# A preLN attention and gated-MLP layer on one core: half of chunk 2's q·k products summed in pairs of tiles by an accumulating transfer, with a new order of steps

## The chip, the cores and the metric

The kernel runs on one core of a Trainium2 chip. The metric is the device time of one execution in microseconds (us), lower is better. It is compared as a median of several runs on the same chip.

## What is computed

```
h  = x + A(layernorm(x))            x: 2048 x 512, bf16
h2 = h + B(layernorm(h))
A: q,k,v = x @ wqkv                 32 heads of 16
   logits[s,w] = q[s] . k[s-2w] / 4      w = 0..7, positions below 0 masked
   o[s] = sum_w softmax(logits)[s,w] v[s-2w];   A = o @ wo
B: gate = x @ W_gate; up = x @ W_up      512 -> 1376
   B = (relu(gate) * up) @ W_down        1376 -> 512
```

## The kernel before

The 2048 positions are cut into four chunks of 512 (`tk` 0 to 3). For each chunk the steps are the same: layernorm, transpose, projection to q, k and v (TensorE, L584), products q·k for eight shifts (VectorE, L635 or L650), sum of these products over the 16 numbers of a head (TensorE, matmul with a matrix `sel` of ones and zeros: "scores", L641, L672 or L693), exponential (L707), denominators (L724), spread of the weights over partitions (eight small transfers per chunk from SyncE, L767), products with v (VectorE, L799 or L814), a tree of additions over the eight shifts (the first level as an accumulating transfer from GpSimd, L842; later levels on VectorE, L802, L836), output projection (TensorE, L880), residual (VectorE, L891), second layernorm (L456, L509), transpose, gate and up (L953; their last 96 columns apart, L920, with a transpose by DMA at L939), and down (L1004).

q and k lie as four tiles of 128 partitions (`t` 0 to 3), where tile t holds 4 of the 16 numbers of all 32 heads. The eight shifts of a chunk are taken in two halves of four (`hf` 0 and 1). For one half VectorE makes the products in two steps of two tiles each; each fills one product buffer, `big`, of 128 x 8 x 512 (1 MB): four shifts for the two tiles. The scores then need 16 matmuls of 128 x 512 against 32 columns each, since both buffers are to be summed. For the halves of chunk 3 (`PRE`) VectorE adds the second buffer to the first (L679), and 8 matmuls do (L693).

Product buffers are scarce: there are five `big` tiles, named big_88 to big_92 below, and the q,k weights' space `wqk_sb` is a sixth once all projections are done. The products with v, the spread weights and the q·k products all draw on them.

The order is written out by a planner. Every step is an `Op` with its engine, its dependencies and its buffers, and the table `RANK` gives each step its place; the planner takes them in that order and emits each engine's instructions in it. Engines then run their queues in order; a step waits for the steps whose results it needs, and for the last reader of a buffer that it overwrites. SyncE and GpSimd only issue transfers here, in queue order too. The tuple `PRD` names the halves (chunk, half) whose two product buffers are to be added by a GpSimd transfer; it is empty before.

The weights for up (`wgu_sb`, L315) and down (`wd_sb`, L309 and L312) are loaded in the middle of the run, from SyncE, after chunk 0's attention has ended.

Of the kernel before, what the change touches and what calls it, by code (L numbers as in the profile page):

```python
# [15 lines left out]


RANK = [
# [38 lines left out]
]  # L57


# [142 lines left out]
def kernel(  # L202
# [22 lines left out]
    BCD = {(0,0):"SSSS",(0,1):"SSSS",(1,0):"SSSS",(1,1):"SSSS",(2,0):"SSSS",(2,1):"SSSS",(3,0):"SSSS",(3,1):"SSSS"}  # L225
    PRE = ((3,0),(3,1))
    PRE2 = ()
    PRD = ()
    ODA = (0, 1)
    LATE = "ud"  # L230
    NAB = 0
# [335 lines left out]
    for tk in range(NCK):  # L567
# [53 lines left out]
        for hf in range(2):  # L621
            sc, ex = Buf(at_s), Buf(ex_s)
            scd, prd = [], []
            for t in range(0, NT, 2):
# [32 lines left out]
                else:  # L657
# [3 lines left out]
                    prd.append((a, pb, f_sc))  # L661
            if (tk, hf) in PRD:
                def f_pd(p0=prd[0][1], p1=prd[1][1]):
                    nc.gpsimd.dma_start(p0.t[:], p1.t[:], accum_op=ALU.add, max_dma_last_dim=4096)
# [429 lines left out]
```

## Time and profile before

| | us |
|---|---|
| median of 3 runs | 192.64 |
| lowest, highest | 192.41, 193.5 |
| the profiled execution, its own time | 193.63 |
| its span, first to last instruction | 191.8 |
| TensorE busy | 185.8 (97%) |
| VectorE busy | 148.3 (77%) |
| ScalarE busy | 115.1 (60%) |
| transfers, 16 engines: SyncE's queue, GpSimd's queue | 30.8%, 25.0% of the span |

All times in this document that have a place ("at 74.05") count from the start of the span. PE is TensorE, DVE VectorE, ACT ScalarE, POOL GpSimd, SP SyncE. Rows of a timeline have start, length, engine, line, operation and tiles, and a count where like instructions in a row were merged; the length of a merged row goes from the first start to the last end. A clock of 1.00 is the full TensorE clock, which the trace shows throughout (mean 0.999).

### The profile page before, as it was taken

Reading aid. Unit: us, or ns where it says so; the run is one execution under the profiler, and the core shown is the slowest. Engines: PE = TensorE matmul, PEld = TensorE weight load, DVE = VectorE, ACT = ScalarE, POOL = GpSimd, SP = SyncE. Lnnn points to the kernel's source line nnn. Section 1 sums busy time; section 2 is a strip of 40 time slices with the busy share of each in tenths; the row PEclk is TensorE's granted clock in tenths of the full one; section 3 lists DMA queues with packets and bytes.
Section 4 is the critical chain, followed back from the end, with each engine's and each line's share of the span. In section 5 each row is a group of like instructions: output and inputs, shape, how many; then the busy total and the mean of one; then the engine's idle time right before and its main releaser. Section 6 shows DMA issues by size and latency. Waiting matters only on the chain.

```text
span 191.8 us, 3035 instructions
## 1 busy us (share of the span) xinstructions
PE 185.8 (97%) x1101; PEld 96.9 (51%) x1120; DVE 148.3 (77%) x230; ACT 115.1 (60%) x236; POOL 18.5 (10%) x35
## 2 busy tenths in 40 slices
PE   7799999999999999999999999999999999999994
PEld 7695455554445354544355444444446444444653
DVE  5799999999999999999999988999627500232433
ACT  2479989997644885793174597615468600656600
POOL 3000002320000033000153000033001000000000
PEclk9999999999999999999999999999999999999999
DMA  5799365993078979628599906689503450000063
GB/s 185 259 329 386 74 158 117 178 191 72 0 198 208 371 157 197 116 43 202 111 166 190 195 20 144 153 157 173 103 0 55 84 164 3 0 27 0 14 215 103
DMA packets 26719, 26.45 MB, mean 138 GB/s; under 512 B 12528, under 2 KB 22608, under 8 KB 26704
## 3 DMA queue, kind: packets, MB, share of 16 engines
q1 hardware_dynamic: 23248, 16.39, 30.8%
q0 software_dynamic: 2736, 8.91, 25.0%
q10 hardware_dynamic: 720, 0.95, 1.6%
q8 instruction: 9, 0.15, 0.3%
q14 instruction: 6, 0.05, 0.1%
HBM read 8.42 MB, written 2.10 MB: 55 GB/s over the span
## 4 chain that ended last, share of the span: by engine, by line
PE 93%; DMA 3%; DVE 1%; issue 1%; SPq 0%
PE bank L953 36%; PE bank L584 21%; PE bank L1004 20%; PE bank L880 7%; DMA x_sm<-in_A_x_dram 3%; PE bank L641 3%; PE bank L920 3%; PE bank L543 2%; PE bank L693 1%; PE bank L724 0%; SPq L323 0%; DVE st L466 0%; DVE row L514 0%; DVE row L1012 0%; DVE mv L469 0%
## 5 line engine op out<-in xcount | busy, mean ns | idle before, releaser
L953 PE MATMUL bank<-quad,wgu_sb 128*128 128x512 bf16 x310 | 71.3, 379 | 0.5
L953 PEld LDWEIGHTS <-wgu_sb 128*128 128x128 bf16 x320 | 30.9, 98 | 37.1 <-issue 1.7
L1004 PE MATMUL bank<-wd_sb,gT 128*128 128x512 bf16 (+3 forms) x195 | 39.4, 355 | 0.2
L960 ACT ACTIVATE gr<-bank 128x512 bf16<-128x512 f32 x40 | 23.5, 609 | 19.4 <-PE bank L953 15.7
L584 PE MATMUL bank<-quad,wqk_sb 128*128 128x512 bf16 (+2 forms) x173 | 30.4, 320 | 1.1 <-DVE quad L557 0.7
L957 ACT CAST up_sb<-bank 128x512 bf16<-128x512 f32 x40 | 23.0, 594 | 13.8 <-PE bank L953 8.7
L981 DVE TENSOR_TENSOR gT<-gr,up_sb 128x1024 bf16<-128x1024 bf16 x20 | 13.7, 688 | 19.4 <-ACT up_sb L957 11.6
L1004 PEld LDWEIGHTS <-gT 128*128 128x128 bf16 (+1 forms) x198 | 18.4, 98 | 19.8 <-issue 0.4
L635 DVE TENSOR_TENSOR big<-quad,kT 128x4096 bf16<-128x4096 bf16 x11 | 24.8, 2282 | 0.1
L584 PEld LDWEIGHTS <-wqk_sb 128*128 128x128 bf16 x176 | 16.9, 114 | 11.9 <-issue 2.1
L842 POOL DMA_DIRECT2D big<-big x13 | 11.8, 958 | 80.4 <-DVE big L799 47.1
L1012 DVE SCALAR_TENSOR_TENSOR row<-bank,iv,x_sm 128x512 bf16<-128x512 f32 (+2 forms) x10 | 6.2, 641 | 13.5 <-PE bank L1004 13.4
L584 PE MATMUL bank<-quad,wv_sb 128*128 128x512 bf16 x61 | 15.6, 379 | 0.2
L880 PE MATMUL bank<-wo_sb,quad 128*128 128x512 bf16 x64 | 14.8, 379 | 0.0
L456 ACT ACTIVATE junk<-x_sm,sm 128x512 bf16<-128x512 bf16 x16 | 11.6, 727 | 4.8 <-DVE x_sm L891 4.8
L799 DVE TENSOR_TENSOR big<-big,vT 128x4096 bf16<-128x4096 bf16 x6 | 13.5, 2283 | 0.2 <-DMA big<-ex 0.2
L802 DVE TENSOR_TENSOR big<-big 128x1024 bf16<-128x1024 bf16 (+2 forms) x19 | 12.2, 656 | 0.7 <-DMA big<-big 0.6
L466 DVE BATCH_NORM_STATS2 st<-x_sm 128x6 f32<-128x512 bf16 x16 | 10.2, 679 | 1.8 <-DMA x_sm<-in_A_x_dram 1.8
L559 ACT COPY quad<-bank 128x1024 bf16<-128x1024 bf16 (+1 forms) x9 | 7.6, 894 | 6.4 <-PE bank L543 6.4
L1010 ACT ACTIVATE up_sb<-bank,iv 128x512 bf16<-128x512 f32 x8 | 5.3, 689 | 10.2 <-PE bank L1004 10.2
L891 DVE SCALAR_TENSOR_TENSOR x_sm<-x_sm,bank 128x512 bf16<-128x512 bf16 x16 | 10.7, 679 | 0.5 <-PE bank L880 0.5
L592 ACT CAST quad<-bank 128x512 bf16<-128x512 f32 x16 | 9.2, 595 | 2.0 <-PE bank L584 1.9
(81 smaller groups left out, 183.9 us busy)
## 6 DMA issues: line engine op xcount, KB each, us to landing
big<-big POOLq DMA_DIRECT2D x13, 512.0 KB, 5.3
big<-ex SPq DMA_DIRECT2D x24, 128.0 KB, 2.7
wgu_sb<-in_B_W_gate_dram SPq DMA_DIRECT2D x1, 1376.0 KB, 11.0
wgu_sb<-in_B_W_up_dram SPq DMA_DIRECT2D x2, 688.0 KB, 4.2
wd_sb<-in_B_W_down_dram SPq DMA_DIRECT2D x2, 640.0 KB, 6.7
x_sm<-in_A_x_dram SPq DMA_DIRECT2D x2, 512.0 KB, 5.9
wqk_sb<-wqk_sb POOLq DMA_DIRECT2D x2, 512.0 KB, 4.8
wqk_sb<-ex SPq DMA_DIRECT2D x8, 128.0 KB, 2.7
```

The costliest lines, as they stand in the source:

```text
L456: nc.scalar.activation(out=junk[:, j % 2, :], in_=h.t[:] if h else x_sm[:, tk * BPC + j, :], func=ACT.Square, bias=sm.t[:, j:j + 1], scale ...
L584: nc.tensor.matmul(mm.t[:, lo:hi], lhsT=wv_sb[:, dt, t:D:NT] if c == 2 else wqk_sb[:, dt, c * D + t:(c + 1) * D:NT], rhs=xnT.t[:, dt, lo:h ...
L635: V.tensor_tensor(out=pb.t[:].rearrange("p (t w) s -> p t w s", t=2), in0=q4, in1=k4, op=ALU.mult)
L799: V.tensor_tensor(out=mt.t[:], in0=ab.t[:], in1=v8, op=ALU.mult)
L802: V.tensor_tensor(out=mt.t[:, 0:n, :], in0=mt.t[:, 0:n, :], in1=mt.t[:, n:2 * n, :], op=ALU.add)
L842: nc.gpsimd.dma_start(mt.t[:, 0:4, :], mt.t[:, 4:8, :], accum_op=ALU.add)
L880: nc.tensor.matmul(od.t[:], lhsT=OT.t[:, t, j * P:(j + 1) * P], rhs=wo_sb[:, t, :], start=(t == 0), stop=(t == NT - 1 and tk not in RPE))
L953: nc.tensor.matmul(mm.t[:fs, lo:hi], lhsT=wgu_sb[:, dt, g, ft * P: ft * P + fs], rhs=hnT.t[:, dt, lo:hi], start=(dt == 0), stop=(dt == NT ...
L957: nc.scalar.copy(out=ub.t[:fs, i, :], in_=um.t[:fs, :])
L960: nc.scalar.activation(out=gr.t[:fs, i, :], in_=gm.t[:fs, :], func=ACT.Relu)
L981: V.tensor_tensor(out=gt.t[:fs, 0:n, :], in0=gr.t[:fs, 0:n, :], in1=ub.t[:fs, 0:n, :], op=ALU.mult)
L1004: nc.tensor.matmul(od.t[:, c0:c1], lhsT=gts[ft].t[:fs, ft % 2, j * P:(j + 1) * P], rhs=wd_sb[:fs, ft, c0:c1], start=(ft == 0), stop=(ft == ...
```

## The change

Half 1 of chunk 2 gets the path named by `PRD`. VectorE still makes its two product buffers. A transfer issued by GpSimd (L664) then adds the second buffer to the first, 1 MB, and the scores of this half are 8 matmuls (L672) where there were 16 (L641). Everything else is computed as before. The table `RANK` is another one throughout: it has one entry more and was searched anew, so that steps on all engines stand in another order.

```
 RANK = [
-    1, 2, 3, 4, 5, 6, 7, 8, 9, 10, 18, 11, 12, 13, 14, 15, 16, 17, 0, 19,
+    0, 1, 2, 3, 4, 5, 6, 7, 8, 9, 18, 10, 11, 12, 13, 15, 16, 17, 14, 19,
...
-    PRD = ()
+    PRD = ((2,1),)
```

The branch that this turns on stood in the code before:

```
if (tk, hf) in PRD:
    def f_pd(p0=prd[0][1], p1=prd[1][1]):
        nc.gpsimd.dma_start(p0.t[:], p1.t[:], accum_op=ALU.add, max_dma_last_dim=4096)
...
    def f_sc(sc=sc, pb=prd[0][1]):
        for u in range(2):
            for g in range(4):
                nc.tensor.matmul(sc.t[g * HB:(g + 1) * HB, :], lhsT=sel[:],
                                 rhs=pb.t[:, 4 * u + g, :], start=(u == 0),
                                 stop=(u == 1), tile_position=(0, g * HB))
```

The rows below are instructions in the order of an engine's queue: line, operation, what is written and read, shape. First GpSimd's queue before, from the four first-level additions of chunk 0 to the four of chunk 1 (L842; each is named by the buffer on which it works):

```order
L842 DMA big_88<-big_88 128x2048
L842 DMA big_89<-big_89 128x2048
L842 DMA big_91<-big_91 128x2048
L842 DMA big_90<-big_90 128x2048
L842 DMA wqk_sb<-wqk_sb 128x2048
L842 DMA big_89<-big_89 128x2048
L842 DMA big_92<-big_92 128x2048
L842 DMA big_90<-big_90 128x2048
```

GpSimd's queue at the same place now:

```order
L842 DMA big_90<-big_90 128x2048
L842 DMA big_88<-big_88 128x2048
L842 DMA big_91<-big_91 128x2048
L842 DMA big_89<-big_89 128x2048
L664 DMA big_92<-big_90 128x2x2048
L842 DMA wqk_sb<-wqk_sb 128x2048
L842 DMA big_89<-big_89 128x2048
L842 DMA big_91<-big_91 128x2048
L842 DMA big_90<-big_90 128x2048
```

The new transfer stands between chunk 0's additions and chunk 1's. It reads big_90, which is also the buffer of chunk 1's last addition.

SyncE's queue before, from the loads of up's weights to the spread of chunk 2's weights (the L939 transpose belongs to chunk 0's gate and up, the first two L767 rows to chunk 1, the last two to chunk 2):

```order
L315 DMA wgu_sb<-in_B_W_up_dram 128x2x1376
L767 DMA big_88<-ex_100 128x1x512 x4
L767 DMA big_88<-ex_102 128x1x512 x4
L315 DMA wgu_sb<-in_B_W_up_dram 128x2x1376
L309 DMA wd_sb<-in_B_W_down_dram 128x5x512 x2
L312 DMA wd_sb<-in_B_W_down_dram 96x512
L939 DMA_TRANSPOSE gT_96<-row_106 128x4x128
L767 DMA wqk_sb<-ex_101 128x1x512 x4
L767 DMA wqk_sb<-ex_100 128x1x512 x4
```

SyncE's queue at the same place now:

```order
L315 DMA wgu_sb<-in_B_W_up_dram 128x2x1376 x2
L767 DMA big_88<-ex_100 128x1x512 x4
L767 DMA big_88<-ex_102 128x1x512 x4
L939 DMA_TRANSPOSE gT_93<-row_104 128x4x128
L309 DMA wd_sb<-in_B_W_down_dram 128x5x512
L312 DMA wd_sb<-in_B_W_down_dram 96x512
L309 DMA wd_sb<-in_B_W_down_dram 128x5x512
L767 DMA big_88<-ex_100 128x1x512 x4
L767 DMA big_88<-ex_101 128x1x512 x4
```

Both halves of up's weights now go ahead of chunk 1's spread, and the loads of down's weights have moved behind the L939 transpose.

VectorE's queue before, from the second product step of chunk 2's half 1 (the first L635 row), over half 0 of that chunk and the four products of chunk 1 with v (L799):

```order
L635 TENSOR_TENSOR big_89<-quad_87,kT 128x4096
L635 TENSOR_TENSOR big_90<-quad_87,kT 128x4096
L635 TENSOR_TENSOR big_91<-quad_87,kT 128x4096
L799 TENSOR_TENSOR wqk_sb<-big_88,vT 128x4096
L799 TENSOR_TENSOR big_89<-big_88,vT 128x4096
L799 TENSOR_TENSOR big_92<-big_88,vT 128x4096
L799 TENSOR_TENSOR big_90<-big_88,vT 128x4096
L981 TENSOR_TENSOR gT_93<-gr_111,up_sb_109 128x1024
L635 TENSOR_TENSOR big_91<-quad_86,kT 128x4096
L802 TENSOR_TENSOR big_89<-big_89 128x1024
L930 TENSOR_TENSOR row_106<-gr_112,bank_143 128x2x96
```

VectorE's queue at the same place now:

```order
L635 TENSOR_TENSOR big_90<-quad_87,kT 128x4096
L635 TENSOR_TENSOR big_89<-quad_87,kT 128x4096
L635 TENSOR_TENSOR big_91<-quad_87,kT 128x4096
L799 TENSOR_TENSOR wqk_sb<-big_88,vT 128x4096
L799 TENSOR_TENSOR big_89<-big_88,vT 128x4096
L799 TENSOR_TENSOR big_91<-big_88,vT 128x4096
L930 TENSOR_TENSOR row_104<-gr_112,bank_142 128x2x96
L799 TENSOR_TENSOR big_90<-big_88,vT 128x4096
L930 TENSOR_TENSOR row_104<-gr_112,bank_138 128x2x96
L739 TENSOR_TENSOR row_106<-ex_101,ex_100 128x512
L981 TENSOR_TENSOR gT_94<-gr_111,up_sb_109 128x1024
L635 TENSOR_TENSOR big_92<-quad_84,kT 128x4096
```

The two L930 rows, after which the L939 transpose can go, now stand around the last product with v, and that product writes big_90, the source of the new transfer.

74 rows, old and new, of the table RANK are left out of this document.

## Prediction

> **What bounds the kernel now.** I read the page's busy shares first, then the chain that ended last, then what TensorE waits for.
>
> ```profile
> PE 185.8 (97%) x1101; PEld 96.9 (51%) x1120; DVE 148.3 (77%) x230; ACT 115.1 (60%) x236; POOL 18.5 (10%) x35
> PE 93%; DMA 3%; DVE 1%; issue 1%; SPq 0%
> PE bank L427 <- DVE warm L327: 1.0, 1, 1.0
> PE bank L584 <- DVE quad L557: 0.7, 1, 0.7
> PE bank L584 <- DMA wqk_sb<-in_A_wqkv_dram: 0.2, 1, 0.2
> ```
>
> The last of these waits, in TensorE's timeline:
>
> ```profile
> 9.27 0.27 PE L584 MATMUL bank<-quad,wqk_sb 128*128 128x128 bf16 x2 [0.72 <-DVE quad L557]
> ```
>
> The chain is 93% TensorE, and the whole list of TensorE's waits is three entries of 1.9 us together, the last of them before 9.27. Behind them TensorE runs without a hole up to its last matmul. So an instruction that leaves TensorE shortens the time by its own length, and a step on any other engine is worth nothing until it comes so late that TensorE waits for it. VectorE is nearly as full in the middle of the run, which says where that could happen:
>
> ```profile
> 60.00:80.00 20.00, 19.89 (x127) 9.34 (x127) 19.69 (x16) 15.07 (x31) 3.45 (x4) 1.00 0.94 226
> 140.00:160.00 20.00, 19.89 (x103) 9.72 (x103) 8.04 (x20) 10.23 (x24) 0.86 (x1) 1.00 0.32 73
> ```
>
> Columns are length, then busy us of TensorE, weight load, VectorE, ScalarE, GpSimd, then clock, transfer share and GB/s. From 60 to 80, where the new transfer goes, TensorE and VectorE have no slack and the transfer engines are 94% busy; from 140 on VectorE and the transfers are mostly idle. A delay between 60 and 80 would show.
>
> **The matmuls that go.** The chain of work in order of time has one run for each half's scores:
>
> ```profile
> 62.16 0.98 PE bank L641 x16
> 65.84 0.98 PE bank L641 x16
> 95.45 0.55 PE bank L693 x8
> ```
>
> The first two are chunk 2's halves with 16 matmuls, the third a half of chunk 3 that already has 8. One half goes from the first form to the third: 0.98 - 0.55 = 0.43 us less on TensorE, all of it on the path.
>
> **The new transfer.** The trace has no 1 MB addition, but it has 512 KB ones of the same kind. GpSimd's timeline, the rate of all transfers from 66 to 82 in slices of 0.4 us with GpSimd's queue in that window, and the landing of the last of chunk 1's four additions, from issue:
>
> ```profile
> 67.45 0.86 POOL L842 DMA_DIRECT2D wqk_sb<-wqk_sb  x1 [28.02 <-DVE wqk_sb L799]
> 74.05 0.86 POOL L842 DMA_DIRECT2D big<-big  x1 [1.34 <-DVE big L799]
> GB/s 381 366 338 200 115 13 0 174 236 236 164 164 246 113 225 225 184 184 215 215 123 225 184 195 215 195 184 195 184 236 205 195 184 133 10 0 0 0 0 0
> q0 software_dynamic: 576, 2.10, 69.6%
> big<-big POOLq DMA_DIRECT2D x1, 512.0 KB, 6.2
> ```
>
> The first is issued at 67.45; the rate falls to zero at 68.4 and starts again at 68.8, so data moves some 1.4 us after issue. It stops in the slice at 79.6, and GpSimd's packets fill 69.6% of the 16 us, 11.1 us: data from 68.8 to some 79.85, 2.77 us for each 512 KB, one behind the other. The last landed at 74.05 + 6.2 = 80.25, 0.4 us after its data. So 1 MB takes 5.5 us, and 1.4 + 5.5 + 0.4 = 7.3 us from issue to landing.
>
> When is it issued, and who waits? VectorE's timeline (start, length):
>
> ```profile
> 58.27 6.68 DVE L635 TENSOR_TENSOR big<-quad,kT 128x4096 bf16<-128x4096 bf16 x3
> 64.87 2.28 DVE L799 TENSOR_TENSOR wqk_sb<-big,vT 128x4096 bf16<-128x4096 bf16 x1
> 67.07 6.68 DVE L799 TENSOR_TENSOR big<-big,vT 128x4096 bf16<-128x4096 bf16 x3
> 73.68 0.68 DVE L981 TENSOR_TENSOR gT<-gr,up_sb 128x1024 bf16<-128x1024 bf16 x1
> 78.35 0.42 DVE L739 TENSOR_TENSOR row<-ex,ex 128x512 bf16<-128x512 bf16 x1
> 80.83 0.41 DVE L836 TENSOR_TENSOR quad<-big 128x512 bf16<-128x512 bf16 x1
> 81.16 0.68 DVE L802 TENSOR_TENSOR big<-big 128x1024 bf16<-128x1024 bf16 x1
> 81.77 0.75 DVE L836 TENSOR_TENSOR quad<-big 128x512 bf16<-128x512 bf16 x2
> 82.77 0.34 DVE L930 TENSOR_TENSOR row<-gr,bank 128x192 bf16<-128x192 bf16 x1
> ```
>
> Lengths overlap the next start by 0.08 (64.87 + 2.28 against 67.07), so I take each 0.08 shorter: L635 and L799 2.20, L981 and L802 0.60, L739 0.34, L836 0.33, L930 0.26. The same VectorE steps lie ahead of the second product step of half 1 in both orders, only shuffled, so I let it start at 58.27 again and end at 60.47. GpSimd issued 0.3 to 0.4 us behind VectorE before (67.45 against the end at 67.07), so the transfer goes at 60.85, its data ends at 67.75 and it lands at 68.2, if nothing else moves. Three things can wait for it:
>
> - Its scores. The new order puts 16 matmuls of half 0, then five groups of four L953 and two of eight L920 ahead of them. The chain gives 8.80 us for 40 of the first and 0.66 us for eight of the second:
>
> ```profile
> 69.51 0.66 PE bank L920 x8
> 70.87 8.80 PE bank L953 x40
> ```
>
> Half 0's products end at 64.87 as before, so these scores start no earlier than 64.87 + 0.98 + 20 x 0.22 + 2 x 0.66 = 71.6. Spare: 3.4 us.
> - The last product with v, which overwrites the transfer's source. VectorE reaches it at 64.87 + 3 x 2.20 + 0.26 = 71.7. Spare: 3.5 us.
> - Chunk 1's four additions, next in GpSimd's queue. The first product with v ends at the same 67.07 as before, so their data would start at 68.8 again. Spare: 1.05 us.
>
> So I cost the transfer at nothing. What covers it is TensorE's work on chunk 0's gate and up. If that cover were gone, the price is 7.3 us less what lies between.
>
> **What the new order moves onto the transfer engines.** This is the doubtful term. Before, the loads of down's weights were issued at 60.6 and had nearly all landed when chunk 1's additions started to move, and the L939 transpose was issued when they were over:
>
> ```profile
> 60.61 1.14 SPq L309 DMA_DIRECT2D wd_sb<-in_B_W_down_dram  x2
> 61.80 0.69 SPq L312 DMA_DIRECT2D wd_sb<-in_B_W_down_dram  x1
> 83.14 1.23 SPq L939 DMA_TRANSPOSE gT<-row  x1
> q1 hardware_dynamic: 1450, 1.82, 102.8%
> wd_sb<-in_B_W_down_dram SPq DMA_DIRECT2D x2, 640.0 KB, 6.7
> wd_sb<-in_B_W_down_dram SPq DMA_DIRECT2D x1, 96.0 KB, 6.9
> ```
>
> Now both stand behind the last L930. VectorE ends that at 64.87 + 4 x 2.20 + 2 x 0.26 = 74.2. The transpose is issued at 74.2 (1.2 us), the loads from 75.5 to 77.3: 1376 KB, in the middle of chunk 1's last two additions. The fourth line is SyncE's queue from 62 to 67, loads alone: 1.82 MB in 5 us, 364 GB/s, so the loads are worth 3.9 us of all engines.
>
> First the loads' own need. Whatever the shares, all of it has moved by 79.85 + 3.9 + some 0.5 for the transpose = 84.3. Down's first matmul stands where it stood, and comes 0.43 us sooner:
>
> ```profile
> 82.97 3.62 PE L880 MATMUL bank<-wo_sb,quad 128*128 128x512 bf16 x16
> 86.42 9.03 PE L1004 MATMUL bank<-wd_sb,gT 128*128 128x512 bf16 x40
> ```
>
> That is 86.0, 1.3 us after the loads landed. No cost.
>
> Then the last addition, whose result goes through three more VectorE steps to the output projection (L880), now at 82.97 - 0.43 = 82.54. VectorE reaches its L802 at 74.2 + 0.34 + 0.60 + 2.20 (L739, L981, L635) + 3 x 0.60 + 2 x 0.33 + 2 x 0.60 (L802, L836, L981) = 81.0, against 80.25 for the landing; from there 0.60 + 2 x 0.33 gives 82.3. So the addition may land 0.75 us later before VectorE waits, and about 0.95 us later before TensorE does. How much later will it land? No row shows such loads and such additions side by side; both ends of the range come from the queues' rows. The loads' data starts about 1 us after issue, at 76.5 (an estimate: a whole 32 KB store lands in 1.5), when 3.35 us of the additions is left.
>
> ```profile
> out_dram<-row ACTq DMA_DIRECT2D x1, 32.0 KB, 1.5
> big<-big POOLq DMA_DIRECT2D x1, 512.0 KB, 4.5
> big<-big POOLq DMA_DIRECT2D x1, 512.0 KB, 4.7
> ```
>
> A packet of the additions takes 0.696 x 16 us x 16 / 576 = 0.309 us of an engine, one of the loads 1.028 x 5 x 16 / 1450 = 0.057 us. If the two queues alternate packet by packet, the loads take 0.057 for each 0.309, and the addition lands 3.35 x 0.18 = 0.6 us late: nothing. If they get equal time, it lands 3.35 us late, and TensorE waits 2.4 us. Less than nothing is excluded, since the loads can only take time away. I take the lower end. The row nearest to it is an addition issued (at 32.58) while transposes from SyncE were in flight: it landed in 4.7 us, against 4.5 us for the one issued at 95.16.
>
> [...]
>
> **The rest of the order.** All engines are shuffled. At the start VectorE waits for the fourth block of x whatever the order:
>
> ```profile
> 8.00 0.69 DVE L466 BATCH_NORM_STATS2 st<-x_sm 128x6 f32<-128x512 bf16 x1 [1.33 <-DMA x_sm<-in_A_x_dram]
> ```
>
> What TensorE can win there is at most its waits of 0.7 and 0.2 us; I take 0. At the end the last matmuls, the last residual and the last store are of the same kinds: 0. In between TensorE has no waits to lose, only to gain.
>
> **Sum.** The profiled execution has 193.63 us, 191.8 of it the span. It becomes 193.63 - 0.43 = 193.2. That execution is 1.0 us above the median of the runs, 192.64, to which I apply the same term: 192.64 - 0.43 = 192.2 us. About 0.5%, 0.96 us, is what a measurement of this kernel can tell from no change, so this gain alone cannot be told.
>
> **Rivals.**
>
> - *The loads hold back chunk 1's last addition* (slower). Place: VectorE waits at the L802 of that addition and TensorE ahead of L880, near 82. It decides when the landing is over 0.95 us late. With turns of equal bytes, a load's turn of 4096 bytes is 0.057 x 4096 / 1255 = 0.186 us (1255 is 1.82 MB / 1450) against 0.309; 3.35 x 0.6 = 2.0 us late, 1.05 us of waiting, 193.3 us. With equal time 2.4 us, 194.6 us. For it: both queues want the same engines, 100% busy before. Against it: packet sizes, and the 4.7. Chance 0.27. [...]
> - *Another step comes late in the new order*, on VectorE, ScalarE or in a queue, by the half microsecond that is the usual spare: 1 us, 193.2 us. For it: VectorE's 19.69 of 20 us. Chance 0.15.
> - *The start gets shorter as well*: the 0.9 us of waits go for the most part, 192.2 - 0.6 = 191.6. Against it: the wait for x stays. Chance 0.10.
> - That the change does not do what it says is hardly possible, since the 8 matmuls are gone from TensorE's queue.
>
> **How the numbers follow.** Forecast 0.48, with its own range 191.8 to 192.7. Faster by over 0.5% is below 191.68: a good half of the third rival, 0.07. Slower is above 193.60: most of the first rival (0.22) and a third of the second (0.05), 0.27. Same: 0.66. The range goes from 191.7 to 194.6: half of the third rival lies below, and what exceeds equal time above.
>
> **What would show it.** Right: 8 matmuls at L672 in about 0.55 us near 72, the new transfer landing about 7.3 us after issue, TensorE's waits still three entries ahead of 10 us. Wrong: an idle stretch of TensorE ahead of L880 near 82 with VectorE waiting for a transfer (first rival), the L672 matmuls or the last L799 waiting for L664, or a first L1004 that waits for `wd_sb`.

## The result, and the profile after

| | before | after |
|---|---|---|
| time, median (9 runs each, same chip) | 192.58 us | 193.95 us |
| ratio, 95% interval | | 1.0076 (1.0058 to 1.0094) |
| profiled execution: time, span | 193.63, 191.8 | 194.2, 191.9 |

The forecast was 192.2. The kernel became 1.4 us slower instead of 0.4 faster, by more than the 0.5% that a measurement can tell.

The page of the changed kernel, busy shares and chain:

```profile
PE 185.5 (97%) x1093; PEld 96.7 (50%) x1112; DVE 148.4 (77%) x230; ACT 115.6 (60%) x236; POOL 19.6 (10%) x36
PE 83%; DMA 7%; DVE 6%; issue 1%; SPq 0%
```

The list of TensorE's waits (total us, times, longest):

```profile
PE bank L880 <- DVE quad L836: 1.1, 1, 1.1
PE bank L427 <- DVE warm L327: 1.0, 1, 1.0
PE bank L584 <- DMA wqk_sb<-in_A_wqkv_dram: 0.3, 1, 0.3
PE bank L543 <- DVE row L514: 0.2, 1, 0.2
```

TensorE's work fell by 8 matmuls, as it should. But the chain is no longer 93% TensorE: transfers and VectorE have entered it, and the list has a new first entry, ahead of chunk 1's output projection. The chain in order of time shows where it left TensorE (start, length):

```profile
73.66 8.12 DMA big<-big
81.80 0.69 DVE big L802
82.49 0.68 DVE quad L836 x2
83.22 3.63 PE bank L880 x16
```

This is the place of the first rival: chunk 1's last addition, issued at 73.66, lands 8.12 us later, and three VectorE steps follow it to TensorE. VectorE's timeline says that it had been ready for 1.35 us, and SyncE's queue what was issued meanwhile:

```profile
81.80 0.69 DVE L802 TENSOR_TENSOR big<-big 128x1024 bf16<-128x1024 bf16 x1 [1.35 <-DMA big<-big]
73.66 2.01 SPq L939 DMA_TRANSPOSE gT<-row  x1
75.72 1.00 SPq L309 DMA_DIRECT2D wd_sb<-in_B_W_down_dram  x1
76.77 1.50 SPq L312 DMA_DIRECT2D wd_sb<-in_B_W_down_dram  x1
78.31 1.61 SPq L309 DMA_DIRECT2D wd_sb<-in_B_W_down_dram  x1
```

The rest went as forecast. The new transfer in GpSimd's timeline and the 8 matmuls that read its result in TensorE's, then its landing from issue:

```profile
60.52 1.20 POOL L664 DMA_DIRECT2D big<-big  x1 [23.00 <-DMA big<-ex]
71.73 0.61 PE L672 MATMUL bank<-big,sel 128*32 128x512 bf16 x8
```

```profile
big<-big POOLq DMA_DIRECT2D x1, 1024.0 KB, 8.5
```

It lands at 69.0, and nothing waits for it.

**A second loss lies outside the span.** The profiled execution has 194.2 - 191.9 = 2.3 us around its span, the one before 1.8. All runs agree: 2.21 to 2.48 in the nine runs of the changed kernel, 1.72 to 1.93 in 102 runs of the kernel before that stood beside the experiments. The queue list of the last stretch has a line that it lacked. Rows of kind `instruction`, before at 145 to 155 us, after at 188 to 198:

```profile
q14 instruction: 1, 0.01, 0.3%
```

```profile
q8 instruction: 1, 0.02, 0.6%
q14 instruction: 1, 0.01, 0.3%
```

I read them as fetches of code. In the kernel before, the q14 fetch is well inside the run (at 150.7) and none follows the last store; after, q14's and q8's start at 192.96 and 193.06, 1.9 and 2.0 us after the last store has landed (191.04) and 1.0 and 1.1 after the last instruction. Which engine's code they are was the second question for the experiments.

### The profile page after: what moved, and what is told of

Read it like the earlier page. It is cut to its first block, busy times and chain, and to the rows that moved or that the text cites. A ratio compares the mean times of both kernels' runs of the same rounds, so it can differ in the third digit from the quotient of the medians.

```text
span 191.9 us, 2995 instructions
## 1 busy us (share of the span) xinstructions
PE 185.5 (97%) x1093; PEld 96.7 (50%) x1112; DVE 148.4 (77%) x230; ACT 115.6 (60%) x236; POOL 19.6 (10%) x36
## 4 chain that ended last, share of the span: by engine, by line
PE 83%; DMA 7%; DVE 6%; issue 1%; SPq 0%
PE bank L953 28%; PE bank L584 21%; PE bank L1004 20%; PE bank L880 7%; DMA big<-big 4%; DMA x_sm<-in_A_x_dram 3%; DVE big L799 3%; PE bank L920 2%; PE bank L641 2%; PE bank L543 2%; DVE wqk_sb L799 1%; PE bank L693 1%; SPq L323 0%; DVE st L466 0%; DVE big L802 0%
## 5 line engine op out<-in xcount | busy, mean ns | idle before, releaser
L953 PE MATMUL bank<-quad,wgu_sb 128*128 128x512 bf16 x310 | 71.7, 379 | 0.5
L953 PEld LDWEIGHTS <-wgu_sb 128*128 128x128 bf16 x320 | 30.9, 98 | 37.3 <-issue 1.7
L1004 PE MATMUL bank<-wd_sb,gT 128*128 128x512 bf16 (+4 forms) x195 | 39.3, 355 | 0.2
L981 DVE TENSOR_TENSOR gT<-gr,up_sb 128x1024 bf16<-128x1024 bf16 x20 | 13.7, 688 | 22.7 <-ACT up_sb L957 11.4
L635 DVE TENSOR_TENSOR big<-quad,kT 128x4096 bf16<-128x4096 bf16 x12 | 27.0, 2280 | 0.0
L799 DVE TENSOR_TENSOR big<-big,vT 128x4096 bf16<-128x4096 bf16 x9 | 20.3, 2281 | 0.0
L842 POOL DMA_DIRECT2D big<-big x13 | 11.6, 894 | 82.1 <-DVE big L799 47.7
L880 PE MATMUL bank<-wo_sb,quad 128*128 128x512 bf16 x63 | 14.9, 379 | 1.1 <-DVE quad L836 1.1
L1012 DVE SCALAR_TENSOR_TENSOR row<-bank,iv,x_sm 128x512 bf16<-128x512 f32 (+2 forms) x10 | 6.2, 641 | 11.8 <-PE bank L1004 11.7
L802 DVE TENSOR_TENSOR big<-big 128x1024 bf16<-128x1024 bf16 (+1 forms) x17 | 10.3, 625 | 2.8 <-DMA big<-big 2.7
L1010 ACT ACTIVATE up_sb<-bank,iv 128x512 bf16<-128x512 f32 x8 | 5.2, 686 | 11.8 <-PE bank L1004 11.8
L880 PEld LDWEIGHTS <-quad 128*128 128x128 bf16 x64 | 6.2, 98 | 8.6 <-DVE quad L836 1.5
```

The source lines that it names most:

```text
L635: V.tensor_tensor(out=pb.t[:].rearrange("p (t w) s -> p t w s", t=2), in0=q4, in1=k4, op=ALU.mult)
L799: V.tensor_tensor(out=mt.t[:], in0=ab.t[:], in1=v8, op=ALU.mult)
L842: nc.gpsimd.dma_start(mt.t[:, 0:4, :], mt.t[:, 4:8, :], accum_op=ALU.add)
L880: nc.tensor.matmul(od.t[:], lhsT=OT.t[:, t, j * P:(j + 1) * P], rhs=wo_sb[:, t, :], start=(t == 0), stop=(t == NT - 1 and tk not in RPE))
L953: nc.tensor.matmul(mm.t[:fs, lo:hi], lhsT=wgu_sb[:, dt, g, ft * P: ft * P + fs], rhs=hnT.t[:, dt, lo:hi], start=(dt == 0), stop=(dt == NT ...
L981: V.tensor_tensor(out=gt.t[:fs, 0:n, :], in0=gr.t[:fs, 0:n, :], in1=ub.t[:fs, 0:n, :], op=ALU.mult)
```

## The experiments

Theories: **L**, the loads of down's weights and the L939 transpose hold back the last addition; **P**, the new 1 MB transfer does it; **F**, GpSimd's program has become too short for its last piece of code to be fetched in good time; **O**, the end is longer for another reason. Each run is compared with runs of the kernel before on the same chip. `X` is the time less the span (median), and the last addition is chunk 1's last L842, from issue to landing.

### Taking the loads and the transpose away, one by one

The first kernel issues the loads at a quiet place near 45 us, by a VectorE write of a few elements into their tile that they must wait for, and the transpose behind the last L836 (shortened):

```
lq = add(("lq",0), "DVE", 0.08, f_lq, [], lat=0.1)      # wd_sb[0:1,:,0:1] = 0, rank 242.5
gh = add(("gh",0), "DVE", 0.08, f_gh, [], take=td.take, lat=0.1)  # gT[0:1,0,0:1] = 0, rank 385.5
td.prio = 385.6; td.deps.append(gh)                     # td: the L939 transpose
if n == "ldd": o.prio, o.deps = 242.6 + 0.1*o.key[1], [lq]
```

> Changed kernel, with the loads of down's weights issued near 45 us, when no transfer runs, and the L939 transpose of chunk 0 held until chunk 1's additions are over (a one-element VectorE write in front of each sets the time). In the changed kernel's profile the last of chunk 1's additions landed 8.1 us after issue (6.2 before) and TensorE waited 1.1 us at L880. Theory T (the transpose takes the transfer engines from the addition): landing back to 6.2 to 6.7 us, no wait at L880, 1.1 us gained, about 192.85 us. Theory L (the loads take them): the same. Theory P (the 1 MB transfer ahead in GpSimd's queue pushes the additions back): landing stays near 8, 193.95 us. Theory O (the loss lies elsewhere in the new order, or outside the span): L880's wait goes but the time stays above 193.4.

The second has the quiet loads and leaves the transpose in its place (without `gh`); the third leaves the loads in the middle of the additions and moves the transpose only:

> Changed kernel, only the loads of down's weights moved to near 45 us; the L939 transpose stays where the change put it, in the middle of chunk 1's last additions. T: the last addition still lands about 8 us after issue, TensorE waits about 1 us at L880, 193.9 us. L: landing 6.2 to 6.7 us, no wait, 192.85 us. P: landing near 8, 193.9 us.

> Changed kernel, only the transpose held back until chunk 1's additions are over; the loads of down's weights go where the transpose went, at 74 us, in the middle of the last two additions. T: landing 6.2 to 6.9 us, wait at L880 below 0.2 us, about 192.9 us, and the loads hardly move until the additions are over. L: landing 8 or more, wait about 1 us, 193.9 us. P: landing near 8.

And the kernel before, as a measure of the scatter:

> The kernel before, once more, for the spans of its single runs: the changed kernel's nine runs had 2.2 to 2.5 us between span and time, the one profiled run of the kernel before 1.8 us. If that part is the kernel's, this one shows 1.8 to 1.9 throughout and about 0.4 us of the loss lies outside the span; if it is the run's, it shows 1.8 to 2.5. Time 192.6 us, ratio 1.000, no wait at L880, last addition of chunk 1 landing in 6.2 us.

| loads | transpose | last addition | wait at L880 | ratio (95%) | X |
|---|---|---|---|---|---|
| among additions | among additions (after) | 8.1 | 1.1 | 1.0076 (1.0058, 1.0094) | 2.29 |
| early | late | 6.2 | none | 1.0021 (0.9994, 1.0047) | 2.30 |
| early | among additions | 7.0 | none | 1.0008 (0.9986, 1.0031) | 2.29 |
| among additions | late | 9.5 | 2.4 | 1.0203 (1.0162, 1.0243) | 2.38 |
| before again | | 6.3 | none | 0.9997 (0.9972, 1.0021) | 1.78 |

The 1.0203 is more than the wait. In the profile of that kernel the granted clock is 0.56 from 85 to 87 us and 0.58 from 87 to 89, right behind the wait, and 1.00 before and after, so that the 16 matmuls of L880 take 5.3 us where they took 3.6; three of its six runs have a mean clock of 0.99. Behind the 1.05 us of waiting in the changed kernel the clock stayed at 1.00. Theory L holds: without both, the addition lands in 6.2 us and the wait is gone. A transpose alone costs the addition 0.8 us, the loads alone 3.3, both together, with the transpose first in SyncE's queue, only 1.9. The queues of the transfer engines show how. The four additions land one behind the other (at 72.5, 75.0, 77.8 and 81.8 in the changed kernel; the third at 78.8 where only the transpose was moved), so the last takes over from the third at about 77 to 79. The kernel with the loads among the additions, at 75.5 to 77.5, 77.5 to 79.5 and 80.5 to 82 (GpSimd's additions are q0, SyncE's transfers q1; records, MB, share of time):

```profile
q0 software_dynamic: 59, 0.24, 111.2%
...
q1 hardware_dynamic: 551, 0.56, 83.0%
q0 software_dynamic: 19, 0.01, 5.8%
...
q0 software_dynamic: 65, 0.27, 88.6%
q1 hardware_dynamic: 61, 0.06, 15.0%
```

In the first 2 us the loads are issued and move nothing yet, but the additions' records already take longer, 0.60 us each (1.112 x 2 x 16 / 59) against 0.31 in the kernel before: 59 of them, where the kernel with early loads and late transpose has 110 in the same window. In the next 2 us the loads have the engines nearly alone. Only then do both queues move side by side, with about as many records each (65 and 61), though a record is 4.1 KB on one queue and 1 KB on the other. The changed kernel at 76.5 to 77.5, 77.5 to 80.5 and 81 to 83:

```profile
q1 hardware_dynamic: 459, 0.12, 69.3%
q0 software_dynamic: 21, 0.03, 33.5%
...
q0 software_dynamic: 121, 0.50, 107.7%
q1 hardware_dynamic: 78, 0.01, 3.2%
...
q1 hardware_dynamic: 747, 0.74, 105.8%
q0 software_dynamic: 4, 0.00, 0.2%
```

Here the transpose, in small records (459 of 0.26 KB), stands first in q1. It has most of the engines for 1 us (69.3% of the time, the additions 33.5%), its last records trickle beside the addition, and the loads behind it hardly move: 0.74 MB of them comes only when the addition is over. So the transpose did harm by itself and kept off a larger one. (The loads are also issued later here, from 75.72 instead of 74.18.) The addition's records also take longer towards its end: 22 from 79.5 to 80.5, where the kernel with early loads and late transpose has 49 in one us. Why one queue first has the engines alone, and why the records get longer, no row shows.

The time of the first kernel came as expected, 192.79 us against 192.85. It is still 0.6 above the forecast, since X stayed at 2.3. The third kernel I had expected at 193.9 us; it took 196.45.

### Lengthening a program

Eight one-element memsets at the end of an engine's program (GpSimd, or VectorE as a control):

```
scr = sb.tile([P, 2], F32, name="scr")
...
for i in range(8):                       # after the last instruction
    nc.gpsimd.memset(scr[0:1, 0:1], 0.0)    # control: nc.vector
```

> The changed kernel with eight one-element memsets more at the end of GpSimd's program, where GpSimd is idle for the last 50 us; nothing else is changed. In the changed kernel the time is 2.3 us above the span (194.2 beside 191.9), in the kernel before 1.8 (193.63 beside 191.8), and its records show an instruction fetch after the last store (queue q14) where the kernel before had that fetch at 150.7 us, some 5 us after GpSimd's 68th record of 75; the changed kernel's GpSimd has 68 records in all. Theory F (fetch): GpSimd's program has become too short to cross the point at which its next piece of code is fetched, so that the runtime's own end after the span waits for it; with eight instructions more the late fetch is gone, time less span falls from 2.3 to 1.8, and the time is 0.45 us below the changed kernel: 193.5, ratio 1.005. Rival O (something else in the new order, or the shorter TensorE program with its own late fetch on q8, makes the end longer): time less span stays at 2.3, time 193.95, ratio 1.0076. Either way chunk 1's last addition still lands 8.1 us after its issue and TensorE still waits 1.1 us at L880.

> The kernel of quiet_loads_late_transpose with the same eight memsets at the end of GpSimd's program. Theory F with theory L (the loads and the transpose are what holds back the last addition): no wait at L880, last addition 6.2 us, span as there (190.4 median, 0.3 below the kernel before), time less span 1.8 instead of 2.3: 192.1 to 192.2, ratio 0.998, which is the forecast of 192.2 come true. Rival O: time less span 2.3, 192.8, ratio 1.002.

> A control: the kernel of quiet_loads_late_transpose with the eight memsets at the end of VectorE's program instead of GpSimd's. Theory F: no change, the late fetch stays, time less span 2.3, time 192.8 (ratio 1.002) or up to 0.3 us more where the memsets lie behind VectorE's last step at the end. Rival (any instructions more do it, or a shift of the program in memory): time less span 1.8, 192.2 to 192.3.

| kernel | X | X in the kernel without the memsets | ratio (95%) |
|---|---|---|---|
| after, GpSimd longer | 1.80 | 2.29 | 1.0048 (1.0032, 1.0065) |
| early loads, late transpose, GpSimd longer | 1.81 | 2.30 | 1.0010 (0.9994, 1.0027) |
| early loads, late transpose, VectorE longer | 2.28 | 2.30 | 1.0019 (1.0000, 1.0038) |

Theory F holds and O falls: eight idle instructions on GpSimd take 0.5 us off X, on VectorE nothing. The ratio fell by 0.0028 in the first kernel and by 0.0011 in the second. The 0.998 that I had expected of the second did not come: its span, 190.5 us, was that of the kernel before on the same chip. The late q14 fetch is now at 130 to 150 us, and q14 has no line behind the last store. Its row in the changed kernel with GpSimd longer, at 130 to 150:

```profile
q14 instruction: 1, 0.01, 0.1%
```

The trace of before has 75 GpSimd records, that of after 68, though the change adds a transfer: the separate semaphore instructions went from 31 to 23 with the new order. With eight memsets there are 76.

TensorE's wait at L880 stays in the first of these kernels (1.5 us in its profile). Two runs tried the same on TensorE, whose program became 16 instructions shorter; X still was 1.96 to 2.46 in 5 of 12 runs of quiet_gpsimd_longer, and 1.95 to 2.56 in 3 of 8 of after_gpsimd_longer. First, eight 128x128 matmuls of zeros at TensorE's end:

> The kernel of quiet_gpsimd_longer (loads early, transpose late, eight memsets at the end of GpSimd's program) with eight 128x128 matmuls of zeros more at the end of TensorE's program, under the last store, so that TensorE's program is as long as before the change. In quiet_gpsimd_longer 5 of 12 runs had time less span at 1.96 to 2.46 and TensorE's last fetch (queue q8) came after the span. Theory F for TensorE's fetch too: that fetch comes some 4 us before the last store's end again, time less span is 1.72 to 1.93 in all runs, and the time is that of the span: 0.2 to 0.3 below the kernel before, ratio 0.9985. Rival: TensorE's fetch costs nothing, time less span still spreads to 2.4, ratio 1.001.

X was 1.73 to 1.84 in all 12 runs, so TensorE's late fetch (q8) costs something too. But the ratio was 1.0049 (1.0018 to 1.0080): the place was badly chosen. The last stores, in this kernel and in the one with GpSimd alone lengthened:

```profile
out_dram<-row SPq DMA_DIRECT2D x1, 64.0 KB, 3.3
out_dram<-row SPq DMA_DIRECT2D x1, 32.0 KB, 3.1
```

```profile
out_dram<-row SPq DMA_DIRECT2D x1, 64.0 KB, 1.5
out_dram<-row SPq DMA_DIRECT2D x1, 32.0 KB, 1.4
```

They land 1.7 us slower, and from chunk 1's L880 to the end of the span it is 109.7 us against 108.7. TensorE's fetch comes at 186.35 there, 0.15 us after the first of these two stores was issued; that it is the fetch that slows them was not tried.

### Each half of the change alone

The new order without the transfer, `PRD = ()` and the scores at ranks 317.5 and 319.5, in two surroundings, and the transfer in the old order:

```
del RANK[453]; RANK[453], RANK[454] = 317.5, 319.5     # new order, no transfer
RANK.insert(453, 301.5); RANK[454], RANK[455] = 341.5, 343.5   # old order, transfer
```

> The new order alone: the changed kernel without its new transfer, the second half of chunk 2's products goes to TensorE unadded in 16 score matmuls, at the place that they had before; the loads of wd and the transpose stand as in the changed kernel. Theory L (the loads and the transpose alone hold back chunk 1's last addition): it lands 8.1 us after its issue as in the changed kernel, TensorE waits 1.1 us at L880, and the 8 matmuls more cost the 0.5 us that quiet_no_transfer showed. GpSimd has one instruction less, so its late fetch falls inside the span's end (0.35 us there, time less span 1.84, as in quiet_no_transfer): in sum about 0.5 above the changed kernel, ratio 1.009 to 1.010. Rival P (the new transfer's 1 MB is what delays the additions): last addition 6.2, no wait at L880, ratio 1.004 as in quiet_no_transfer.

> The kernel of quiet_loads_late_transpose without the new transfer: the second half of chunk 2's products goes to TensorE unadded again, in 16 score matmuls instead of 8; the scores stand where the kernel before has them. It has the new order, the loads of wd and the late transpose. What the transfer is worth by itself, where nothing holds back chunk 1's last addition: the prediction's sum says 0.43 us of TensorE and no cost for the transfer, so the span is 0.43 above that of quiet_loads_late_transpose, at 190.85 (median). Rival (the transfer slows the chunk's other additions or the scores wait for it): under 0.2 us difference. Time less span: 1.8 if GpSimd's code again crosses its fetch, 2.3 if not: time 192.6 or 193.2.

> The transfer alone: the order of the kernel before, with only the new transfer put on GpSimd behind the last product of chunk 2 and its 8 score matmuls moved to where the changed kernel has them. Here the three loads of wd are issued at 60.6 to 61.8, at the same time as the new transfer, and the additions of chunk 1 are alone in the queues (6.2 us as before). The transfer lands 8.5 us after its issue if the loads do not hold it back, and 11.8 if they do as much as they did with the addition (3.3 us), that is at 69 to 72.3. Theory L: the scores, at about 72, and the last multiplication at L799, at 71.4, which takes the transfer's source buffer, wait for nothing or up to 0.9 us; that multiplication's addition has about 1 us of spare. So TensorE's 0.43 us is kept, wholly or in most: ratio 0.998, at worst 1.001; GpSimd's program is long enough, time less span 1.8. Rival (the transfer needs the new order): a wait of over 1 us at the scores or at L880, ratio above 1.003.

> The kernel of old_order_transfer with the same eight matmuls at the end of TensorE's program. If TensorE's late fetch costs something: 0.1 us less than old_order_transfer in the median, time less span 1.8 with no run above 1.95; if not, the same time. By theory L the ratio is 0.9975 to 0.998, which would be the version that beats both kernels.

The new order alone: ratio 1.0070 (1.0046 to 1.0095), the last addition in 7.4 us, TensorE's wait still there:

```profile
PE bank L884 <- DVE quad L840: 0.9, 1, 0.9
```

So P falls: the loss needs no new transfer. With early loads and no transfer the last addition lands in 5.2 us, with the transfer in 6.2, so the loads and the transpose cost 2.2 us of landing without the transfer and 1.9 with it. L had expected 8.1 and 0.5 us more than the changed kernel, 1.009 to 1.010; that much more did not come, the interval just reaches it. With early loads the kernel without the transfer has 1.0036 (1.0017 to 1.0056) and a span of 191.3 us, 0.9 above the one with it (190.4). In both kernels without it GpSimd has 69 records, and X is 1.84 and 1.86, but from chunk 1's L880 to the end it is 109.05 us in their profiles, 0.35 more than the 108.7 with the transfer. With eight memsets on GpSimd (quiet_no_transfer_longer below) it is 108.7 again, so these 0.35 us hang on the length of GpSimd's program too; that its last instruction waits there for the fetch is argued, since the q14 record itself comes only behind the span (191.42 in quiet_no_transfer). That leaves some 0.55 us for the transfer's worth.

The old order with the transfer is the worst of all: 1.0237 (1.0195 to 1.0279), where I had expected 0.998 and 1.001 at worst. With TensorE lengthened as above X fell from 1.93 to 1.80, but the time did not: 1.0263 (1.0227 to 1.0299). TensorE's largest wait, and the landings between 55 and 90 (behind this wait, too, the granted clock was low: 0.50 from 73 to 75 and 0.66 from 75 to 77):

```profile
PE bank L676 <- DMA big<-big: 2.1, 1, 2.1
```

```profile
big<-big POOLq DMA_DIRECT2D x3, 512.0 KB, 10.4
wd_sb<-in_B_W_down_dram SPq DMA_DIRECT2D x2, 640.0 KB, 12.5
big<-big POOLq DMA_DIRECT2D x1, 1024.0 KB, 13.0
```

I had expected 11.8 at most, from the 3.3 us that the loads cost a 512 KB addition. They cost the 1 MB transfer 4.5, and in their turn were held back themselves (12.5 against 6.7 before). The transfer, issued at 59.82, starts late. The queues at 61.5 to 65.5 and at 66 to 78:

```profile
q1 hardware_dynamic: 814, 1.01, 91.8%
...
q0 software_dynamic: 567, 2.14, 89.2%
q1 hardware_dynamic: 586, 0.57, 17.1%
```

First SyncE's loads move alone for 4 us, then both queues move with about as many records each (567 and 586), as above. The new transfer does need the loads out of its way; the new order put them into the next one's.

### Both losses removed

The early loads and the late transpose, GpSimd lengthened, and eight one-column matmuls in TensorE's warm-up (`nc.tensor.matmul(wb.t[:, 0:1], lhsT=warm[:], rhs=warm[:, 0:1], ...)`); and the same kernel without transfer and without that padding, which it doesn't need:

> The kernel of quiet_gpsimd_longer (loads of wd early, transpose late, eight memsets at the end of GpSimd's program) with eight one-column matmuls of zeros more in the warm-up at TensorE's start, where it waits 0.5 to 0.9 us for the first row at L543 anyway, so that TensorE's program is as long as before the change. If the saved 0.43 us reach the time: time less span 1.8 in all runs, span 190.2 to 190.3 beside 190.6 of the kernel before, 192.1, ratio 0.998; if something in the new order eats it: ratio 1.000 to 1.001 again, with a span of 190.5.

> The kernel of quiet_no_transfer with eight memsets at the end of GpSimd's program, so that its late fetch goes (0.35 us at the end of the span there): the new order with loads early and transpose late, and no transfer. Beside quiet_padded_start it differs by the transfer alone: 16 score matmuls instead of 8. If the transfer's saving reaches the time, it is 0.43 to 0.53 us above quiet_padded_start: 192.6, ratio 1.0005; if not, level with it.

| kernel | time | ratio (95%) | span | X |
|---|---|---|---|---|
| with the transfer | 191.64 | 0.9959 (0.9940, 0.9979) | 189.8 | 1.80 |
| without it | 192.63 | 1.0005 (0.9990, 1.0020) | 190.8 | 1.81 |

The first beats both kernels, by 0.8 us that of before, and by more than the 0.998 that I had expected. Not all of it is the transfer's: without the padded warm-up (quiet_gpsimd_longer) the ratio was 1.0010 and the span 190.5 us, level with the kernel before, and only 0.3 below the 190.8 without the transfer (on another chip). TensorE's one wait in the first is the one at its start:

```profile
PE bank L428 <- DVE warm L328: 1.0, 1, 1.0
```

The two spans differ by 1.0 us, more than the transfer's work. TensorE's timelines give 0.53 us for the stretch in which they differ, from the first L953 block to chunk 1's L880: 60.41 to 80.95 with it, 61.17 to 82.24 without, 20.54 against 21.07.

```profile
60.41 3.62 PE L956 MATMUL bank<-quad,wgu_sb 128*128 128x512 bf16 x16
80.95 3.40 PE L883 MATMUL bank<-wo_sb,quad 128*128 128x512 bf16 x15
```

```profile
61.17 3.62 PE L957 MATMUL bank<-quad,wgu_sb 128*128 128x512 bf16 x16
82.24 2.12 PE L884 MATMUL bank<-wo_sb,quad 128*128 128x512 bf16 x9
```

The other half lies ahead of 60, where TensorE waits for the first rows (1.7 us at L547 in the second profile, nothing in the first). Whether the padded warm-up helps there or the arrival of x, which scatters (VectorE waits 1.8 us for it in one profile of the kernel before, 0.3 in the other), is open.

## Why the prediction was wrong, step by step

- **The matmuls that go, 0.43 us: right.** From chunk 0's first L880 to chunk 1's, the kernel before takes 30.49 us (50.93 to 81.42 in before_again), the one with early loads and late transpose 30.28 (50.80 to 81.08). One L724 matmul of 0.22 us moved into that stretch, so like for like 30.71 became 30.28: 0.43. Without the transfer it is 30.81, 0.53 more. The L880 rows of before_again, then of the kernel with early loads and late transpose:

```profile
50.93 1.89 PE L880 MATMUL bank<-wo_sb,quad 128*128 128x512 bf16 x8
81.42 1.89 PE L880 MATMUL bank<-wo_sb,quad 128*128 128x512 bf16 x8
```

```profile
50.80 1.03 PE L880 MATMUL bank<-wo_sb,quad 128*128 128x512 bf16 x4
81.08 2.10 PE L880 MATMUL bank<-wo_sb,quad 128*128 128x512 bf16 x9
```

- **The new transfer costs nothing: right in the result, short in the size.** Issue 60.52 (60.85 forecast), landing 8.5 us later (7.3), its scores at 71.73 (71.6), nobody waits. But most of the 1.05 us that I gave chunk 1's additions as spare was used: with early loads the first of them landed in 5.5 us, against 4.6 without the transfer.
- **The doubtful term is the step that failed: "I take the lower end."** I had 0.6 and 3.35 us for how much later the last addition lands, and took the first, packet by packet. It was 1.9 us, and 1.35 us of it VectorE waited, 1.1 TensorE. Where both queues moved, their records were about equal in number (65 to 61), as in that working, so the shares behind the 0.6 us were right there. What the working left out is the stretch ahead of them, in which one queue has the engines nearly alone (2 us for the loads, 1 us for the transpose), and that the addition's records get longer. It also put no price on the transpose for the addition, which was 0.8 us. The row that I leaned on, an addition that landed in 4.7 us beside transposes, said nothing on loads and did not hold for this transpose. Loads alone cost 3.3 us, close to the equal time that I had as the other end, and TensorE's 2.4 us of waiting with them is what I had worked out for it; but no row shows equal time, so this fit is luck. The point of decision, 0.95 us, was right: 0.8 us (the transpose alone) gave no wait, 1.9 gave 1.1.
- **The rival that came true** had 2.0 us late, 1.05 us of waiting and 193.3 us at equal bytes. The two sizes fit by luck and not for its reason: the loads, which it spoke of, were kept off by the transpose in front of them until the addition was over, and turns of equal bytes stand in no row above.
- **"The profiled execution becomes 193.63 - 0.43" left out a term.** It took the 1.8 us around the span as fixed. They became 2.3, because the new order made GpSimd's program 7 records shorter.
- **The start and the end, 0: nearly right.** From chunk 1's L880 to the end of the span it is 108.7 us in six of the nine kernels with the new order and the transfer (109.1 with VectorE lengthened, 109.7 with the slow stores, 110.4 with the low clock behind the long wait), 108.8 and 109.0 in the two profiles of before. The start scatters: chunk 0's first L880 starts at 52.47 and 50.93 in the two profiles of before, at 51.72 in the changed kernel.

The sum as measured: -0.43 for the matmuls and 1.22 for the late addition (31.50 us from L880 to L880 in the changed kernel's profile against 30.28) are 0.79 inside the span, and 0.5 outside make 1.3, of the 1.4 in the medians.

## What to carry to other kernels

A reorder that frees a queue for one transfer moves other transfers into a later one: list, for every moved issue, what else is in flight there, and where no row shows the two together, take neither end for the forecast but ask how much of the range lies beyond the decision point: here 0.95 us in a range from 0.6 to 3.35. The shares that I worked out did not say who goes first: bulk loads cost a 512 KB accumulating transfer 3.3 us here and a 1 MB one 4.5, and had the engines nearly alone for 2 and 4 us before both queues moved, and a small transfer in front of the loads in their queue brought the 3.3 down to 1.9. And compare the time less the span, not the span alone: half a microsecond was outside it, and eight idle instructions brought it back.

## What the runs showed of the hardware that was not expected

- The queues of the transfer engines have rows of kind `instruction` while the program runs (9 on q8 and 6 on q14 in the kernel before), which I read as fetches of code. Where the last q14 row came only behind the last store, the end was longer: by 0.5 us behind the span with 68 GpSimd records, by 0.35 us inside it with 69; with 75 to 77, where that row came 40 to 55 us earlier, by nothing.
- A 1 MB accumulating transfer from GpSimd landed in 8.4 to 8.6 us without loads beside it, and in 13.0 and 13.7 with 1376 KB of loads issued at the same time.
- Of two queues with data, one first had the engines nearly alone, then both moved with about as many records each, 1 KB on one queue and 4.1 KB or 3.8 on the other: loads 551 records to 19 in 2 us, then 61 to 65; 814 to none in 4 us, then 586 to 567.
- Behind a wait of TensorE of 2.4 and 2.1 us in mid-run the granted clock was 0.50 to 0.66 for 4 us; behind waits of 1.05 and 1.5 us it stayed at 1.00.
